# The row bias, the sum's epsilon and half of the top-k comparisons of the first fourteen attention units, moved to GpSimd

## The chip, the core and the metric

One Trainium2 chip, one core. The metric is the device time of one execution in microseconds (us). A core has a matrix engine (TensorE; its matmuls are "PE" in the profile, its weight loads "PEld"), a vector engine (VectorE, "DVE"), an engine for activation functions (ScalarE, "ACT"), a general-purpose engine (GpSimd, "POOL") and an engine that here only issues transfers (SyncE, "SP"). Each takes its instructions in order; an instruction that waits holds up everything behind it on its engine. Arrays are tiles of 128 partitions times a number of elements.

## What is computed

Three stages in a chain: attention that keeps the 32 largest scores of each row, a mixture of eight experts weighted by a Sinkhorn-balanced gate, and a second feed-forward with a Mish-like activation. Only the first concerns the change:

```python
scores = scale * (q @ k.T)                      # 2 batches, 8 heads, 576 x 576, head size 64
kth = np.partition(scores, -32)[..., -32:-31]   # 32nd largest of each row
scores = np.where(scores >= kth, scores, -1e9)
attn = np.exp(scores - scores.max(-1))
attn = attn / (attn.sum(-1) + 1e-9)
x = attn @ v                                    # then experts, then the second feed-forward
```

## The kernel before

The 1152 rows (two batches of 576) are nine token tiles of 128. A **unit** is one tile and one head, 72 in all; units 0 to 7 are tile 0, units 8 to 15 are tile 1, and so on. The expert stage runs in three chunks of tiles, (0, 1), (2, 3) and (4 to 8), so it can begin when unit 15 is done; what it needs of later tiles is computed beside it.

A unit goes through five steps. `scores` multiplies on TensorE into one PSUM tile and ScalarE copies it to `s` (L235). `threshold` finds the 32 largest of each row on VectorE: four times MAX8 (L254, eight largest into `top`) with three MATCH_REPLACE8 between (L261, which strike those eight out of the copy `w`). `mask` and the exponential follow in one of two ways. The units after the first `POOL_UNITS` = 13 take the exponential of the raw scores early, and one VectorE instruction (L290) compares, multiplies and sums. The first 13 units, called pooled here, take the other way:

- VectorE writes -3e38 where a score is below the 32nd largest, else 0 (L285, the comparison).
- GpSimd adds the scores to it (L286).
- VectorE multiplies the row's maximum by -0.125 into `nb` (L271, the bias), one number per partition.
- ScalarE takes the exponential with that bias and sums the row into `sm` (L272).

`norm` adds 1e-9 to the sum on VectorE (L299), takes the reciprocal on VectorE (L300), and ScalarE scales the row (L305). `values` transposes on TensorE, copies on ScalarE (L328, L339), multiplies by the values, and after a tile leaves `xh`/`xl`, the two parts of the expert stage's input (L362 to L367).

The small tiles `top`, `nb`, `sm` and `r` have four buffers each: the bias of unit u+4 can be written when the exponential of unit u has read its own. `s` has six buffers, `em` three pairs.

TensorE's order is written out by hand: at step i of `attention` the scores of unit i come first, then the values of unit i-5 for a pooled unit (i-4 for the others), then two units of early scores of tiles 2, 3, 5 and 6, whose halves ScalarE copies out (L239). So the scores of unit u+6 stand on TensorE behind the values of unit u. The order on the other engines is set by a planner from stream priorities and its own estimates of when each operand is ready. Two streams matter: what stands in `moe` comes behind `attn` (L299 and L300 of pooled units are put there), and weight preparation of the later pieces (`prep`) comes ahead of `attn`.

GpSimd also makes the low parts of keys and queries (L158, L188), clears query tiles (L179), and makes the low parts of the first expert weights (L522), which are loaded ahead and first used when the expert stage begins. Units of tile 2 are held on VectorE until the reciprocal of unit 15 (the "ends" in `threshold` and `norm`).

Of the kernel before, what the change touches and what calls it, by code (L numbers as in the profile page):

```python
# [14 lines left out]
ALU = mybir.AluOpType  # L15
# [20 lines left out]
NEG = -3.0e38  # L36
SCALE = 0.125
EPS = 1e-9
# [5 lines left out]
LAG = 2  # L44
LAG2 = 2
AHEAD = 2
POOL_UNITS = 13
EARLY = [(t, h) for t in (2, 3) for h in range(H)] + [(t, h) for t in (5, 6) for h in range(HG)]
EARLY_FROM, EARLY_PER_STEP = 5, 2
HOLD, RATE = 8, 0.25  # L50
# [22 lines left out]
def attention_moe_moe2(ctx: ExitStack, tc: tile.TileContext, qT, kT, vm, vt, wg, wst, w64, out):  # L73
    nc = tc.nc
# [5 lines left out]
    def after(inst, earlier):  # L80

        tc.add_manual_dep(
            inst.ins,
            earlier.ins.name,
            mybir.DependencyInfo(mybir.DependencyClass.NoSync, mybir.DependencyReason.DATA),
            reason="order",
        )
# [180 lines left out]
    def exponential(t, h, dst, src, eng, **kw):  # L268

        nb = small.tile([P, 1], F32, tag="nb", name=f"nb_{t}_{h}")  # L270
        eng.tensor_scalar(nb, live["top", t, h][:, 0:1], -SCALE, None, op0=ALU.mult)  # L271
        nc.scalar.activation(dst, src, AF.Exp, bias=nb, scale=SCALE, **kw)  # L272
        return dst

    def mask(t, h, on_pool):

        with st("attn"):
            s = live.pop(("s", t, h))
            sm = small.tile([P, 1], F32, tag="sm", name=f"sm_{t}_{h}")
            kth = live["top", t, h][:, TOPK - 1 : TOPK]  # L280
            if h % 2 == 0:
                live["pair", t, h] = sp.tile([P, 2 * S], F32, tag="em", name=f"em_{t}_{h}", bufs=3)
            em = live["pair", t, h - h % 2][:, h % 2 * S :][:, :S]
            if on_pool:
                nc.vector.tensor_scalar(em, s, kth, NEG, op0=ALU.is_lt, op1=ALU.mult)  # L285
                nc.gpsimd.tensor_tensor(em, em, s, ALU.add)  # L286
                exponential(t, h, em, em, nc.vector, accum_out=sm)
            else:
                e = live.pop(("e", t, h))
                nc.vector.scalar_tensor_tensor(em, s, kth, e, op0=ALU.is_ge, op1=ALU.mult, accum_out=sm)  # L290
            live["em", t, h], live["sm", t, h] = em, sm
        yield from ()

    def norm(t, h, on_pool):
        with st("attn"):
            em, sm = live["em", t, h], live.pop(("sm", t, h))
            r = small.tile([P, 1], F32, tag="r", name=f"r_{t}_{h}")
            with st("moe" if on_pool else "attn"):
                nc.vector.tensor_scalar(r, sm, EPS, None, op0=ALU.add)  # L299
                inv = nc.vector.reciprocal(r, r)  # L300
            if (t, h) == (CHUNKS[0][-1], H - 1):
                live["ends"] = inv
                for inst in live.pop("held", ()):
                    after(inst, inv)
            nc.scalar.activation(em, em, AF.Copy, scale=r)  # L305
        yield from ()
# [96 lines left out]
    def attention():  # L403
# [10 lines left out]
        for u, (t, h) in enumerate(units):  # L414
            pooled = u < POOL_UNITS
            for order, (stage, delay) in enumerate(
                (
                    (scores, 0),
                    (partial(threshold, on_pool=pooled), AHEAD),
                    (partial(mask, on_pool=pooled), AHEAD + 1),  # L420
                    (partial(norm, on_pool=pooled), AHEAD + (2 if pooled else 1)),
                    (values, AHEAD + (3 if pooled else 2)),
                )
            ):
                plan.setdefault(u + delay, []).append((order, u, partial(stage, t, h)))
# [420 lines left out]
```

## Time and profile before

| | |
|---|---|
| median of 3 runs | 1249.01 us (1248.32 to 1250.55) |
| the profiled execution's own time | 1249.09 us |
| its span, first to last instruction | 1247.3 us |
| busy over the span | PE 95%, PEld 83%, DVE 69%, ACT 52%, POOL 44% |
| mean granted TensorE clock | 0.993 of full speed |

How to read it: the span has stages. Up to about 107 us there is attention of tiles 0 and 1 alone; from there to about 500 us expert work and the rest of attention run together; then the last expert chunk, and the second feed-forward. Shares over the whole span mix these, so the rows below are taken by stretch. A line such as L285 is a line of the kernel before.

### The profile page before, as it was taken

The numbers are of one execution on the slowest core, as the hardware profiler recorded it, in microseconds if no ns is written. First come the engines' busy times: TensorE is split into PE (matmuls) and PEld (weight loads), VectorE is DVE, ScalarE is ACT, GpSimd is POOL, SyncE is SP. The second block draws the span as 40 slices with busy tenths as digits, with TensorE's granted clock in tenths as the row PEclk, the third lists the DMA queues.
The fourth block names the chain that finished last, engine by engine and source line by source line (L and its number), as shares of the span: only waits on it lengthen the run. The fifth ranks groups of instructions, "written<-read, shape, count | busy, mean of one in ns | idle before, by whom it ended". The sixth has DMA issues, their size and how long they took to land.

```text
span 1247.3 us, 20676 instructions
## 1 busy us (share of the span) xinstructions
PE 1180.1 (95%) x7267; PEld 1040.7 (83%) x7267; DVE 858.7 (69%) x1857; ACT 648.1 (52%) x1289; POOL 546.8 (44%) x424
## 2 busy tenths in 40 slices
PE   3678999999999999999999988999999999999998
PEld 2566888998889888889888777899999998889997
DVE  6999999999999999534899989952333332323221
ACT  6786777877777777653233333332323333444432
POOL 7844778877877777771112211121111212222110
PEclk9899999999999999999999999999999999999999
DMA  8444555575655555673278776632222231223201
GB/s 254 121 144 148 178 168 173 178 223 170 213 178 167 163 155 160 186 219 120 79 249 267 237 217 205 217 100 76 77 76 73 72 110 54 91 93 119 76 27 43
DMA packets 105113, 183.18 MB, mean 147 GB/s; under 512 B 14128, under 2 KB 24624, under 8 KB 105008
## 3 DMA queue, kind: packets, MB, share of 16 engines
q1 hardware_dynamic: 103712, 180.68, 46.6%
q8 instruction: 57, 0.93, 0.3%
q10 hardware_dynamic: 1296, 1.18, 0.3%
q14 instruction: 48, 0.39, 0.1%
HBM read 158.55 MB, written 23.27 MB: 146 GB/s over the span
## 4 chain that ended last, share of the span: by engine, by line
PE 66%; DVE 24%; DMA 6%; issue 2%; POOL 1%; ACT 1%; SPq 0%; POOLq 0%; ACTq 0%; DVEq 0%
PE h_c2e L619 12%; PE y_c2e L596 11%; PE h_d L619 8%; PE y_d L596 8%; PE y_c0e L596 7%; PE h_c0e L619 7%; DVE top L254 6%; DVE w L261 5%; PE h_c1e L619 4%; PE y_c1e L596 3%; DMA cx<-in_w_dram 3%; DVE em L290 2%; DVE acc L640 2%; PE pv L348 2%; PE tr L325 1%
## 5 line engine op out<-in xcount | busy, mean ns | idle before, releaser
L522 POOL TENSOR_TENSOR wl_c2e<-wraw_c2e,wh_c2e 128x512 fp32r<-128x512 f32 x64 | 90.7, 1417 | 358.8 <-ACT wh_c2e L520 332.0
L522 POOL TENSOR_TENSOR wl_c1e<-wraw_c1e,wh_c1e 128x512 fp32r<-128x512 f32 x128 | 172.5, 1372 | 52.4 <-ACT wh_c1e L520 49.3
L522 POOL TENSOR_TENSOR wl_c0e<-wraw_c0e,wh_c0e 128x512 fp32r<-128x512 f32 x128 | 171.6, 1356 | 53.0 <-ACT wh_c0e L520 49.9
L619 PE MATMUL h_c2e<-xh,wh_c2e 128*128 128x320 f32 x512 | 161.3, 315 | 14.4 <-DVE hl_c2e L538 14.2
L520 ACT ACTIVATE wh_c2e<-wraw_c2e 128x512 fp32r<-128x512 f32 x128 | 80.7, 630 | 174.5 <-PE y_c2e L596 110.3
L619 PE MATMUL h_c2e<-xl,wh_c2e 128*128 128x320 f32 x512 | 158.7, 310 | 0.0
L619 PE MATMUL h_c2e<-xh,wl_c2e 128*128 128x320 f32 x512 | 158.5, 310 | 0.0
L254 DVE MAX8 top<-w 128x8 f32<-128x576 f32 x216 | 157.7, 747 | 0.8
L596 PE MATMUL y_c2e<-wh_c2e,hh_c2e 128*128 128x512 f32 x320 | 126.6, 396 | 0.5 <-DVE acc L640 0.5
L596 PE MATMUL y_c2e<-wl_c2e,hh_c2e 128*128 128x512 f32 x320 | 125.7, 393 | 0.0
L596 PE MATMUL y_c2e<-wh_c2e,hl_c2e 128*128 128x512 f32 x320 | 125.2, 391 | 0.0
L538 DVE SCALAR_TENSOR_TENSOR hl_c2e<-h_c2e,hh_c2e 128x320 fp32r<-128x320 f32 x128 | 62.1, 485 | 87.2 <-ACT hh_c2e L537 87.0
L619 PEld LDWEIGHTS h_c2e<-xh,wh_c2e 128*128 128x128 f32 x512 | 96.6, 189 | 24.0 <-DVE hl_c2e L538 21.9
L522 POOL TENSOR_TENSOR wl_d<-wraw_d,wh_d 128x512 fp32r<-128x512 f32 x32 | 41.4, 1293 | 161.0 <-ACT wh_d L520 161.0
L520 ACT ACTIVATE wh_c0e<-wraw_c0e 128x512 fp32r<-128x512 f32 x128 | 80.4, 629 | 51.9 <-PE y_c0e L596 21.0
L261 DVE MATCH_REPLACE8 w<-top,w 128x576 f32<-128x576 f32 x144 | 106.3, 740 | 0.0
L619 PEld LDWEIGHTS h_c2e<-xl,wh_c2e 128*128 128x128 f32 x512 | 96.6, 189 | 1.8
L557 DVE TENSOR_TENSOR hl_d<-mg_d,hh_d 128x320 fp32r<-128x320 f32 (+1 forms) x48 | 31.5, 657 | 95.7 <-ACT hh_d L556 95.7
L619 PEld LDWEIGHTS h_c2e<-xh,wl_c2e 128*128 128x128 f32 x512 | 96.7, 189 | 0.0
L520 ACT ACTIVATE wh_c1e<-wraw_c1e 128x512 fp32r<-128x512 f32 x128 | 79.8, 627 | 27.7 <-PE y_c1e L596 11.3
L522 DVE TENSOR_TENSOR wl_c2e<-wraw_c2e,wh_c2e 128x512 fp32r<-128x512 f32 x64 | 47.7, 745 | 66.0 <-ACT wh_c2e L520 65.9
L520 ACT ACTIVATE wh_d<-wraw_d 128x512 fp32r<-128x512 f32 x64 | 40.4, 631 | 95.8 <-PE y_d L596 40.9
(170 smaller groups left out, 3325.5 us busy)
## 6 DMA issues: line engine op xcount, KB each, us to landing
wraw_c0e<-in_wst_dram SPq DMA_DIRECT2D x128, 256.0 KB, 3.0
wraw_c1e<-in_wst_dram SPq DMA_DIRECT2D x128, 256.0 KB, 3.0
wraw_c2e<-in_wst_dram SPq DMA_DIRECT2D x128, 256.0 KB, 2.9
cx<-in_w_dram SPq DMA_DIRECT2D x32, 512.0 KB, 4.6
wraw_d<-w SPq DMA_DIRECT2D x64, 256.0 KB, 2.7
yd<-ysp SPq DMA_DIRECT2D x32, 256.0 KB, 3.6
yb<-yd SPq DMA_DIRECT2D x32, 256.0 KB, 3.4
w<-cc SPq DMA_DIRECT2D x32, 256.0 KB, 3.2
```

What stands on the lines that cost most here:

```text
L254: top8 = nc.vector.max(g, src)
L261: nc.vector.match_replace(w, g, src, NEG)
L290: nc.vector.scalar_tensor_tensor(em, s, kth, e, op0=ALU.is_ge, op1=ALU.mult, accum_out=sm)
L325: nc.tensor.transpose(tr[:, c, :], em[:, j * D + c * P :][:, :P], ident)
L348: nc.tensor.matmul(pv[i * D : (i + 1) * D, pair, c0:c1], vmain[b, pair][:, i, c, :], live["at", i][:, c, c0:c1], start=(c == 0), stop=False,)
L520: nc.scalar.activation(hi, raw, AF.Copy)
L522: eng.tensor_sub(lo, raw, hi)
L538: nc.vector.scalar_tensor_tensor(l, ps, 0.0, h, op0=ALU.max, op1=ALU.subtract)
L557: nc.vector.tensor_sub(l, g, h)
L596: nc.tensor.matmul(y, h[:, j * P : (j + 1) * P], w, start=(f == 0 and k == 0), stop=(f == nf - 1 and k == 2),)
L619: nc.tensor.matmul(ps, w[:, c * P : (c + 1) * P], x[:, c, c0 : c0 + m], start=(k == 0), stop=(k == 3 * NC - 1),)
L640: nc.vector.scalar_tensor_tensor(acc[t], y, gate[:, t, e : e + 1], acc[t], op0=ALU.mult, op1=ALU.add)
```

## The change

`POOL_UNITS` becomes 14, so unit 13 (tile 1, head 5) takes the pooled way too. In pooled units the bias and the epsilon go to GpSimd, and so does the comparison of even heads; odd heads keep it on VectorE. The reciprocal stays on VectorE, the streams and TensorE's written order stay as they are (the values of unit 13 move from step 17 to step 18).

```diff
-POOL_UNITS = 13
+POOL_UNITS = 14
...
             if on_pool:
-                nc.vector.tensor_scalar(em, s, kth, NEG, op0=ALU.is_lt, op1=ALU.mult)
+                flags = nc.vector if h % 2 else nc.gpsimd
+                flags.tensor_scalar(em, s, kth, NEG, op0=ALU.is_lt, op1=ALU.mult)
                 nc.gpsimd.tensor_tensor(em, em, s, ALU.add)
-                exponential(t, h, em, em, nc.vector, accum_out=sm)
+                exponential(t, h, em, em, nc.gpsimd, accum_out=sm)
...
             with st("moe" if on_pool else "attn"):
-                nc.vector.tensor_scalar(r, sm, EPS, None, op0=ALU.add)
+                (nc.gpsimd if on_pool else nc.vector).tensor_scalar(r, sm, EPS, None, op0=ALU.add)
                 inv = nc.vector.reciprocal(r, r)
```

## Rows read from the trace of the kernel before

**Rows 1.** The page: share of the chain that ended last, by engine.
```profile
PE 66%; DVE 24%; DMA 6%; issue 2%; POOL 1%; ACT 1%; SPq 0%; POOLq 0%; ACTq 0%; DVEq 0%
```

**Rows 2.** Busy time by stretch: stretch, length, busy us (count) of each engine, clock, DMA.
```profile
7.30:107.60 100.30, 62.43 (x372) 49.10 (x373) 96.14 (x240) 76.20 (x169) 63.45 (x51) 0.93 0.57 175
107.60:488.00 380.40, 377.61 (x2798) 337.46 (x2797) 374.78 (x906) 283.66 (x556) 294.89 (x221) 1.00 0.56 173
```

**Rows 3.** Waits of TensorE from 107.6 us on: total, times, longest.
```profile
PE h_c2e L619 <- DVE hl_c2e L538: 14.2, 16, 2.0
```

**Rows 4.** The chain that ended last, 40 to 56 us: start, us, what.
```profile
41.64 0.77 ACT em L272 x2
...
42.44 0.15 DVE nb L271
```

**Rows 5.** Groups on VectorE, 7.3 to 107.6 us: count | busy, mean ns | idle before.
```profile
L254 DVE MAX8 top<-s 128x8 f32<-128x576 f32 x16 | 11.9, 746 | 3.1 <-ACT s L235 2.9
...
L285 DVE TENSOR_SCALAR em<-s,top 128x576 f32<-128x576 f32 x13 | 8.9, 687 | 0.0
...
L290 DVE SCALAR_TENSOR_TENSOR em<-s,top,e 128x576 f32<-128x576 f32 x3 | 2.4, 802 | 0.0
...
L271 DVE TENSOR_SCALAR nb<-top 128x1 f32<-128x1 f32 x17 | 2.3, 140 | 3.0 <-ACT em L272 3.0
...
L299 DVE TENSOR_SCALAR r<-sm 128x1 f32<-128x1 f32 x16 | 2.2, 137 | 0.0
```

**Rows 6.** VectorE in order of time: start, us, instruction, [idle before].
```profile
25.98 0.15 DVE L271 TENSOR_SCALAR nb<-top 128x1 f32<-128x1 f32 x1 [2.68 <-ACT em L272]
...
37.29 0.70 DVE L285 TENSOR_SCALAR em<-s,top 128x576 f32<-128x576 f32 x1
...
60.79 0.76 DVE L254 MAX8 top<-s 128x8 f32<-128x576 f32 x1
61.47 0.07 DVE L261 MATCH_VALUE_LOAD w<-top,w 128x8 f32 x1
61.53 0.74 DVE L261 MATCH_REPLACE8 w<-top,w 128x576 f32<-128x576 f32 x1
62.19 0.08 DVE L261 MATCH_VALUE_LOAD w<-top,s 128x8 f32 x1
...
62.92 0.14 DVE L271 TENSOR_SCALAR nb<-top 128x1 f32<-128x1 f32 x1
62.98 1.41 DVE L254 MAX8 top<-w 128x8 f32<-128x576 f32 x2
64.30 0.14 DVE L299 TENSOR_SCALAR r<-sm 128x1 f32<-128x1 f32 x1
64.36 0.52 DVE L285 TENSOR_SCALAR em<-s,top 128x576 f32<-128x576 f32 x1
64.78 0.09 DVE L261 MATCH_VALUE_LOAD w<-top,w 128x8 f32 x1
```

**Rows 7.** ScalarE in order of time: the copy of unit 9's scores.
```profile
60.11 0.65 ACT L235 ACTIVATE s<-sc 128x576 f32<-128x576 f32 x1
```

**Rows 8.** Busy time by stretch, as in rows 2, within the first stage.
```profile
7.30:25.30 18.00, 6.62 (x20) 4.91 (x20) 14.87 (x33) 8.84 (x16) 13.61 (x12) 1.00 0.89 263
25.30:55.00 29.70, 16.87 (x82) 13.25 (x84) 28.73 (x69) 23.70 (x52) 28.85 (x21) 0.91 0.60 179
55.00:107.60 52.60, 38.95 (x274) 30.94 (x271) 52.53 (x139) 43.66 (x103) 21.00 (x18) 0.92 0.44 143
```

**Rows 9.** GpSimd in order of time: the addition of unit 3.
```profile
44.52 1.65 POOL L286 TENSOR_TENSOR em<-em,s 128x576 f32<-128x576 f32 x1
```

**Rows 10.** Groups on GpSimd, 7.3 to 107.6 us, as in rows 5.
```profile
L286 POOL TENSOR_TENSOR em<-em,s 128x576 f32<-128x576 f32 x13 | 19.0, 1461 | 8.8 <-DVE em L285 6.4 <-DVE r L299 2.3
...
L522 POOL TENSOR_TENSOR wl_c0e<-wraw_c0e,wh_c0e 128x512 fp32r<-128x512 f32 x9 | 11.8, 1333 | 1.4 <-ACT wh_c0e L520 1.1
L179 POOL MEMSET qraw<- 128x512 f32 x4 | 2.1, 528 | 0.1
...
L411 POOL TENSOR_TENSOR wgs<-wgraw,wgs 128x32 fp32r<-128x32 f32 x1 | 0.3, 252 | 0.1
```

## The prediction

> **What bounds the kernel now.** I read the chain that ended last first: 66% of the span on TensorE, 24% on VectorE, GpSimd 1% [rows 1]. Then busy time by stretch, since these shares mix stages. Up to 107.6 us, before the first expert matmul, VectorE is busy 96.14 of 100.30 us and TensorE 62.43: VectorE sets the pace. From 107.6 to 488 us TensorE is busy 377.61 and VectorE 374.78 of 380.40, so both are full there [rows 2]. After 107.6 us the largest wait of TensorE is 14.2 us in 16 pieces, all on VectorE's low parts in the last expert chunk [rows 3]. Nothing in the later stages waits for a fixed moment, so what the first stage gains or loses should pass to the end one for one, and the question is by how much unit 15 ends earlier.
>
> Inside the first stage I read the engines by thirds. VectorE is nearly full in the last two (28.73 of 29.70 and 52.53 of 52.60). GpSimd is full as well from 25.3 to 55 us, 28.85 of 29.70, and only 21.00 of 52.60 afterwards [rows 8]. And the chain goes, at 42.44 us, from ScalarE's exponential to VectorE's bias [rows 4]: VectorE was waiting there, for a buffer of the bias that the exponential four units earlier was still to read.
>
> **What leaves VectorE.** The durations overlap by some hundredths, so I cost by the distance to the next start, and between 60.79 and 64.78 us every kind is to be seen: a bias 0.06 us (62.92 to 62.98), an epsilon 0.06 (64.30 to 64.36), a comparison 0.42 against a duration of 0.52 [rows 6].
> - Bias: 14 units (unit 13 included) by 0.06 = 0.84 us. Epsilon: 14 by 0.06 = 0.84 us.
> - Comparisons of even heads: units 0, 2, 4, 6, 8, 10, 12, seven by the group's mean of 0.687 less 0.10 of overlap = 4.1 us [rows 5, 6].
> - Unit 13 loses its combined instruction, 0.802 less some 0.08 of overlap, and gets a comparison of 0.42: 0.3 us [rows 5, 6].
> - VectorE waits 3.0 us in front of biases, 2.68 of it at 25.98 us, when the bias of unit 4 waits for unit 0's exponential [rows 5, 6]. The wait moves to GpSimd with the bias; VectorE goes on to the comparison of unit 1, which needs nothing from it: 3.0 us.
>
> Together 9.1 us by which VectorE could be ahead. This is a gross figure. What is late next is the arrival of scores.
>
> **What of it can be used.** VectorE works on several units at a time; this hides late scores. The stock runs down, however. Unit 9's scores are copied out at 60.11 + 0.65 = 60.76 us [rows 7], and VectorE takes them at 60.79 [rows 6]. What it still has of unit 8 then is one MATCH_REPLACE8 with its load (61.47 to 62.19, 0.72) and one of the two MAX8 at 62.98 (0.66): 1.4 us, apart from the comparison. So if unit 9's scores come no earlier than now, a VectorE that is ahead does these 1.4 us before, and then idles. After that point it saves only what is still to come: biases of units 9 to 13, 0.30; epsilons of 7 to 13, 0.42; comparisons of units 8, 10, 12 at 0.42 = 1.26; unit 13, 0.3. That is 2.3, and with the 1.4 it makes 3.7 us. The lead is therefore 3.7 us with the scores of unit 9 standing still, 9.1 at most if they come early enough, and less by every us that they come later.
>
> **What is added to GpSimd, and whether the scores stand still.** Scores of unit u+6 stand behind the values of unit u on TensorE, and these need GpSimd's addition. In 25.3 to 55 us GpSimd has no room: unit 3's comparison ends on VectorE at 37.99 and its addition starts at 44.52 [rows 6, 9], behind other work of the queue. Into this stretch come two comparisons (units 2 and 4; unit 0's falls before 25.3 us, where GpSimd is idle 4.4 of 18.0 us), five biases and five epsilons.
> - One comparison on GpSimd is not in the trace. Below it lies a write-only fill, 0.528 us for 512 elements, 0.59 for 576; above it the two-input addition of the same size, 1.461 [rows 10]. One input is read, two operations are done: I take 1.0, and as a far bound twice the addition, 2.9.
> - A 128x1 operation: at most 0.252, that of 128x32 [rows 10]; at least what VectorE takes, 0.06 [rows 6]. I take 0.2.
>
> That is 2 x 1.0 + 10 x 0.2 = 4.0 us more in a full queue (1.8 to 8.3 by the bounds). Against it, VectorE hands the comparison of unit 1 over 2.7 us earlier and that of unit 3 some 3 to 4 us earlier, and nine weight preparations, 11.8 us [rows 10], stand in this stage though the first is used at 107.6 us; the planner can let them give way. I take these as equal: the scores of unit 9 stay where they are. After 55 us GpSimd has 31 us of idle time, which hides the other comparisons, the small work and unit 13's addition; without that cover each comparison of an even unit would put its 1.0 us less VectorE's 0.42 into the way from threshold to addition. A wait is new there: GpSimd's bias waits for an exponential, and its epsilon for a sum, with key parts and additions queued behind them; VectorE's reciprocal waits for GpSimd. Against the epsilon's place on VectorE I count this at zero, from -1 to +2 us.
>
> One page of the Trainium skill, SBUF — State Buffer, section "Who interferes with whom", says that a VectorE instruction in a two-port mode and a GpSimd instruction exclude each other for the whole instruction. The trace agrees in kind: the comparison takes 0.52 at 64.36 and 0.687 in the mean [rows 5, 6]. By that rule the seven comparisons left on VectorE would meet more GpSimd work; were each 0.2 us longer, the sum would fall by 1.4 us to 2.3.
>
> **The sum.** The profiled execution took 1249.09 us, 0.08 above the median, with 1.8 outside its span. 1249.09 - 3.7 = 1245.4; against the median 1245.3. I predict 1245.3.
>
> **The rivals.**
> A. My forecast: scores of unit 9 within about 2 us of now, 1243 to 1247.5. Chance 0.40.
> B. The scores come early too: weight preparation gives way, and the earlier comparisons pull exponentials, values and scores with them. For it speaks that VectorE was tied with the chain at 42 us [rows 4]; against it GpSimd's full queue [rows 8]. The whole 9.1 us: 1240.0. Chance 0.20.
> C. The added 4.0 us push every addition of the full stretch by as much: 3.7 - 4.0 = -0.3 us, 1249.4, no change. Chance 0.22.
> D. GpSimd becomes the bound of the first 60 us because its comparison is dear. At the far bound 2 x 2.9 + 10 x 0.25 = 8.3 us, and 3.7 - 8.3 = -4.6: 1253.7, slower. It decides from the point where the added work passes 3.7 + 2.5 us, a comparison of 2.1 us. For it: GpSimd's two-input operation already takes 1.461 where VectorE's one-input comparison takes 0.52. Against it: the fill takes 0.528, and only one input is read. Chance 0.18. The Trainium skill, GPSIMD Engine Reference, section "Engine selection", would have elementwise work on VectorE, though it calls one-input work on GpSimd about as fast as the line allows; its section "Elementwise — side-by-side cycle accounting" puts data-dependent branching at some 12 cycles an element at 1.2 GHz, which for 576 elements would be, as an estimate, 5.8 us a comparison and, by the same sum, about 10 us more time than now. No row here shows a comparison on GpSimd.
>
> **How the numbers follow.** Below 0.2%, 2.5 us, this kernel can't be told from unchanged. Faster: B, most of A, 0.56 together; same: the rest of A, most of C, 0.25; slower: most of D and a little of C, 0.19. The range from 1239.5 to 1252 takes in B, A, C and the nearer part of D. Within the likeliest case it is 1243 to 1247.5.
>
> **What would show it.** Right: seven comparisons left on VectorE and no wait in front of a bias; seven on GpSimd at about 1.0 us each; VectorE idle a few us in front of first MAX8s between 45 and 65 us; the first expert matmul 3 to 4 us before 107.6, and every later stage shifted by as much. Case B: VectorE without idle time and the first expert matmul near 98.5 us. Case C: GpSimd full to about 59 us and the first expert matmul where it is. Case D: a comparison of over 2.1 us. The prediction fails on its premise if the expert stage starts earlier and the end does not follow, for instance because the planner orders the later stages differently.

## The result, and the profile after

The changed kernel takes 1267.68 us (median of 4 runs, 1264.81 to 1268.74) against 1249.78 beside it: ratio 1.014, 95% interval [1.0118, 1.0162]. It is 17.5 us slower; the forecast was 1245.3, with a range from 1239.5 to 1252. Here and below a difference in us is the ratio less one, times the median of the kernel before in the same comparison. One slow execution each of two runs below (1496.92 and 2957.98 us) is left out of their ratios. Rows of a trace are those of one execution, which in the runs below took up to 4.4 us more or less than the median of its kernel, so differences of a few us between two traces can be chance. In the changed kernel every line from 286 on has a number one higher: the comparison is L286, the addition L287, the epsilon L300, the reciprocal L301, the low part L523.

The first look is where the stage ends. The first expert matmul, in TensorE's order of time (start, us, instruction), before and after:

```profile
107.63 0.37 PE L619 MATMUL h_c0e<-xh,wh_c0e 128*128 128x256 f32 x1
```
```profile
124.72 0.37 PE L620 MATMUL h_c0e<-xh,wh_c0e 128*128 128x256 f32 x1
```

That is 17.1 us later, and the span grew from 1247.3 to 1264.9, by 17.6: the loss arises in the first stage and passes on. The second look is busy time by stretch, as in [rows 8]:

```profile
7.30:25.30 18.00, 6.64 (x20) 4.90 (x20) 17.05 (x34) 9.26 (x16) 15.47 (x17) 1.00 0.87 267
25.30:55.00 29.70, 9.41 (x51) 7.55 (x51) 22.99 (x46) 16.99 (x34) 28.58 (x24) 0.97 0.49 155
55.00:107.60 52.60, 33.50 (x211) 27.91 (x211) 38.92 (x86) 38.20 (x90) 34.41 (x40) 0.76 0.26 86
```

From 25.3 to 55 us GpSimd (last of the five busy times) is full, as before, and every other engine has fallen: VectorE from 28.73 to 22.99, TensorE from 16.87 to 9.41. After 55 us GpSimd does 34.41 in place of 21.00. TensorE's granted clock (the first number behind the busy times) is 0.76 there in place of 0.92; whether that is a cause is taken up with the experiments. The page's shares of the chain that ended last, which answer to [rows 1], have GpSimd at 4% for 1%:

```profile
PE 61%; DVE 24%; DMA 7%; POOL 4%; issue 2%; ACT 1%; SPq 0%; POOLq 0%; ACTq 0%
```

In order of time that chain is on GpSimd, with gaps for issue only, from 27.49 to 66.2 us. In [rows 4] it had gone over to VectorE at 42.44.

The new operations, as groups on GpSimd up to 130 us (count | busy, mean ns | idle before), and the comparisons left on VectorE up to 117 us:

```profile
L287 POOL TENSOR_TENSOR em<-em,s 128x576 f32<-128x576 f32 x14 | 19.6, 1409 | 3.1 <-DVE em L286 2.6
L286 POOL TENSOR_SCALAR em<-s,top 128x576 f32<-128x576 f32 x7 | 15.9, 2265 | 0.7 <-DVE top L254 0.2
...
L300 POOL TENSOR_SCALAR r<-sm 128x1 f32<-128x1 f32 x14 | 3.2, 227 | 5.7 <-ACT em L272 4.2 <-PE sc L226 0.8
L271 POOL TENSOR_SCALAR nb<-top 128x1 f32<-128x1 f32 x14 | 3.1, 225 | 3.8 <-DVE top L254 3.1
```
```profile
L286 DVE TENSOR_SCALAR em<-s,top 128x576 f32<-128x576 f32 x7 | 6.1, 867 | 0.1
```

A comparison takes 2.27 us on GpSimd, longer than the addition of two inputs. What it does to the queue is read on GpSimd in order of time:

```profile
28.86 2.50 POOL L523 TENSOR_TENSOR wl_c0e<-wraw_c0e,wh_c0e 128x512 fp32r<-128x512 f32 x2
31.44 1.40 POOL L158 TENSOR_TENSOR ks<-kraw,ks 64x576 fp32r<-64x576 f32 x1
32.92 3.81 POOL L523 TENSOR_TENSOR wl_c0e<-wraw_c0e,wh_c0e 128x512 fp32r<-128x512 f32 x3
36.81 1.41 POOL L158 TENSOR_TENSOR ks<-kraw,ks 64x576 fp32r<-64x576 f32 x1
38.30 0.21 POOL L271 TENSOR_SCALAR nb<-top 128x1 f32<-128x1 f32 x1
38.57 0.21 POOL L300 TENSOR_SCALAR r<-sm 128x1 f32<-128x1 f32 x1
38.88 2.24 POOL L286 TENSOR_SCALAR em<-s,top 128x576 f32<-128x576 f32 x1
...
52.63 2.76 POOL L287 TENSOR_TENSOR em<-em,s 128x576 f32<-128x576 f32 x2
...
59.57 2.42 POOL L286 TENSOR_SCALAR em<-s,top 128x576 f32<-128x576 f32 x1
61.96 1.26 POOL L188 TENSOR_TENSOR q<-qraw,q 128x512 fp32r<-128x512 f32 x1
63.31 0.24 POOL L271 TENSOR_SCALAR nb<-top 128x1 f32<-128x1 f32 x1
63.61 0.22 POOL L300 TENSOR_SCALAR r<-sm 128x1 f32<-128x1 f32 x1
```

and ScalarE beside it (unit 0's sum, unit 2's exponential, unit 8's scores; the copy of unit 8's scores before stands below):

```profile
30.30 0.19 ACT L272 ACTIVATION_READ_ACCUMULATOR em<-em,nb 128x1 f32 x1
...
55.42 0.78 ACT L272 ACTIVATE em<-em,nb 128x576 f32<-128x576 f32 x1 [2.61 <-POOL em L287]
...
72.31 0.66 ACT L235 ACTIVATE s<-sc 128x576 f32<-128x576 f32 x1
```
```profile
52.22 0.63 ACT L235 ACTIVATE s<-sc 128x576 f32<-128x576 f32 x1
```

Follow two units. Unit 0's sum is there at 30.49, and its epsilon, 0.21 us of work, runs at 38.57: ahead of it in the queue stand low parts of expert weights first used after 107 us, two key parts and a bias. Unit 2's comparison runs at 38.88; its addition is the second of the pair at 52.63, so it ends at 55.39. Before, the addition ended at 40.49, and the epsilon ran on VectorE at 42.51:

```profile
39.08 1.41 POOL L286 TENSOR_TENSOR em<-em,s 128x576 f32<-128x576 f32 x1
```
```profile
42.51 0.14 DVE L299 TENSOR_SCALAR r<-sm 128x1 f32<-128x1 f32 x1
```

The addition is 14.9 us later. The epsilon then comes at 63.61, behind a key part, unit 4's addition, a comparison, two query parts and a bias. So it is 21.1 us late, 14.9 by the addition and 6.2 by what comes after it, and unit 2's scaled row starts 19.7 us late, at 64.12 for 44.44. The scores of unit 8, which TensorE does behind the values of unit 2, are in SBUF at 72.97 for 52.9 before: 20.1 late. The waits of VectorE and of TensorE, 7.3 to 117 us (total, times, longest), say the same from the other side; the last row is TensorE's wait before:

```profile
DVE r L301 <- POOL r L300: 12.6, 7, 4.0
DVE top L254 <- ACT s L235: 9.4, 6, 2.4
```
```profile
PE tr L326 <- ACT em L306: 32.8, 3, 19.0
```
```profile
PE tr L325 <- ACT em L305: 14.9, 6, 8.1
```

TensorE's wait for the scaled row grew by 17.9, the size of the loss.

### The profile page after: what moved, and what is told of

Its sections match the earlier page's. It is cut to its first block, busy times and chain, and to the rows that moved or that the text cites. A ratio compares the mean times of both kernels' runs of the same rounds, so it can differ in the third digit from the quotient of the medians.

```text
span 1264.9 us, 20684 instructions
## 1 busy us (share of the span) xinstructions
PE 1179.6 (93%) x7267; PEld 1041.4 (82%) x7267; DVE 859.1 (68%) x1821; ACT 650.6 (51%) x1290; POOL 568.6 (45%) x460
## 4 chain that ended last, share of the span: by engine, by line
PE 61%; DVE 24%; DMA 7%; POOL 4%; issue 2%; ACT 1%; SPq 0%; POOLq 0%; ACTq 0%
PE h_c2e L620 11%; PE y_c2e L597 10%; PE h_d L620 8%; PE y_d L597 8%; PE h_c0e L620 7%; PE y_c0e L597 6%; DVE top L254 5%; DVE w L261 5%; DMA cx<-in_w_dram 4%; PE y_c1e L597 3%; DVE em L291 3%; PE h_c1e L620 2%; PE pv L349 2%; DMA yb<-yd 2%; DVE acc L641 2%
## 5 line engine op out<-in xcount | busy, mean ns | idle before, releaser
L523 POOL TENSOR_TENSOR wl_c2e<-wraw_c2e,wh_c2e 128x512 fp32r<-128x512 f32 x64 | 93.3, 1459 | 353.9 <-ACT wh_c2e L521 322.9
L523 POOL TENSOR_TENSOR wl_c1e<-wraw_c1e,wh_c1e 128x512 fp32r<-128x512 f32 x128 | 171.9, 1366 | 54.3 <-ACT wh_c1e L521 51.2
L523 POOL TENSOR_TENSOR wl_c0e<-wraw_c0e,wh_c0e 128x512 fp32r<-128x512 f32 x128 | 169.5, 1335 | 57.1 <-ACT wh_c0e L521 54.0
L620 PE MATMUL h_c2e<-xh,wh_c2e 128*128 128x320 f32 x512 | 161.2, 315 | 12.6 <-DVE hl_c2e L539 12.4
L620 PEld LDWEIGHTS h_c2e<-xh,wh_c2e 128*128 128x128 f32 x512 | 96.6, 189 | 21.8 <-DVE hl_c2e L539 19.7
L523 POOL TENSOR_TENSOR wl_d<-wraw_d,wh_d 128x512 fp32r<-128x512 f32 x32 | 41.4, 1293 | 161.0 <-ACT wh_d L521 161.0
L523 DVE TENSOR_TENSOR wl_c2e<-wraw_c2e,wh_c2e 128x512 fp32r<-128x512 f32 x64 | 48.1, 752 | 65.0 <-ACT wh_c2e L521 64.9
```

Of the source, the lines that this page charges most:

```text
L523: eng.tensor_sub(lo, raw, hi)
L620: nc.tensor.matmul(ps, w[:, c * P : (c + 1) * P], x[:, c, c0 : c0 + m], start=(k == 0), stop=(k == 3 * NC - 1),)
```

## The experiments

The accounts to be told apart: the loss is GpSimd's added time (the comparison is simply long); it is one misplaced part, the epsilon above all; or it is order, that is, short and urgent operations standing in one queue behind long ones that nobody waits for. The marker "first expert matmul" is 107.63 in the kernel before.

**One part alone.** Epsilon on GpSimd:

```diff
-                nc.vector.tensor_scalar(r, sm, EPS, None, op0=ALU.add)
+                (nc.gpsimd if on_pool else nc.vector).tensor_scalar(r, sm, EPS, None, op0=ALU.add)
```

> Only the epsilon of the 13 pooled units is on GpSimd; bias and comparisons stay on VectorE. Three theories of the 18 us. Price: GpSimd's comparison takes 2.24 us and fills it; then this kernel, without it, is within 2.5 us of before (1247 to 1251). Epsilon: its 0.2 us stands behind 1.3 to 1.4 us operations in GpSimd's queue and VectorE's reciprocal waits (12.6 us of such waits in the changed kernel); then this alone costs 8 us or more (1257 to 1265). Order: the addition of an even unit is placed far behind its comparison (unit 2's 12.8 us later); then this is near before as well, up to 4 us slower.

Measured: 1255.33 against 1248.82, ratio 1.0049 [1.0034, 1.0063], +6.1 us; first expert matmul 113.67. On ScalarE unit 1's sum is there at 32.00, and on GpSimd, in order of time:

```profile
31.82 0.18 ACT L272 ACTIVATION_READ_ACCUMULATOR em<-em,nb 128x1 f32 x1
```
```profile
32.23 4.03 POOL L522 TENSOR_TENSOR wl_c0e<-wraw_c0e,wh_c0e 128x512 fp32r<-128x512 f32 x3
36.34 1.40 POOL L158 TENSOR_TENSOR ks<-kraw,ks 64x576 fp32r<-64x576 f32 x1
37.81 1.37 POOL L522 TENSOR_TENSOR wl_c0e<-wraw_c0e,wh_c0e 128x512 fp32r<-128x512 f32 x1
39.26 0.21 POOL L299 TENSOR_SCALAR r<-sm 128x1 f32<-128x1 f32 x1
```

An operation of 0.21 us comes 7.3 us after its operand. The loss lies between the two branches that were expected, below the 8 us of the epsilon's and above the 2.5 and 4 us of the others. It is more than the thirteen operations last, some 3 us together. Unit 7's scores, behind the values of unit 1, are at 51.1 for 46.8.

The bias on GpSimd:

```diff
-                exponential(t, h, em, em, nc.vector, accum_out=sm)
+                exponential(t, h, em, em, nc.gpsimd, accum_out=sm)
```

> Only the bias of the 13 pooled units is on GpSimd. All three theories (price, epsilon, order) put little here. My prediction's own term says 3.0 us of waits and 0.8 us of work leave VectorE: 1246 to 1249. If the wait for the exponential four units earlier merely stops GpSimd in VectorE's stead, 1250 to 1253.

Measured: 1251.07, ratio 1.0014 [1.0002, 1.0026], +1.7 us; first expert matmul 109.61. A small loss, in the range expected if the wait merely moves: VectorE now waits 4.4 us in front of epsilons, for 3.0 in front of biases before.

The comparison of even heads on GpSimd:

```diff
-                nc.vector.tensor_scalar(em, s, kth, NEG, op0=ALU.is_lt, op1=ALU.mult)
+                flags = nc.vector if h % 2 else nc.gpsimd
+                flags.tensor_scalar(em, s, kth, NEG, op0=ALU.is_lt, op1=ALU.mult)
```

> Only the comparison of the seven even pooled units is on GpSimd. Price: 2 x 2.24 us more in the full stretch up to 55 us, 4 to 6 us slower than before at most, with additions right behind their comparisons. Order: additions of units 2 and 4 again stand several operations behind their comparisons, and this alone brings most of the loss, 1259 to 1268. Epsilon: within 3 us of before.

Measured: 1260.19, ratio 1.0084 [1.0065, 1.0103], +10.5 us, in the range expected of order; first expert matmul 119.79. GpSimd in order of time, comparisons of units 2 and 4 and additions of units 3 and 2:

```profile
39.94 2.21 POOL L286 TENSOR_SCALAR em<-s,top 128x576 f32<-128x576 f32 x1
42.12 1.42 POOL L287 TENSOR_TENSOR em<-em,s 128x576 f32<-128x576 f32 x1
...
47.85 2.20 POOL L286 TENSOR_SCALAR em<-s,top 128x576 f32<-128x576 f32 x1
50.14 1.40 POOL L158 TENSOR_TENSOR ks<-kraw,ks 64x576 fp32r<-64x576 f32 x1
51.61 1.40 POOL L287 TENSOR_TENSOR em<-em,s 128x576 f32<-128x576 f32 x1
```

Unit 2's addition starts 9.5 us after its own comparison has ended on the same engine, behind unit 3's addition, two low parts, unit 4's comparison and two key parts.

Fourteen units in place of thirteen:

```diff
-POOL_UNITS = 13
+POOL_UNITS = 14
```

> Only the number of pooled units, 13 to 14; all operations stay where they were. No theory puts any of the loss here: 1247 to 1251.

Measured: 1250.94, ratio 1.001 [0.9995, 1.0025], +1.2 us, not told from none. The four alone add to 6.1 + 1.7 + 10.5 + 1.2 = 19.5, all together cost 17.5.

**One part taken back.** The changed kernel with the epsilon on VectorE (the first diff, reversed):

> The changed kernel with the epsilon alone back on VectorE. If the parts add up (epsilon 6.1, bias 1.8, comparisons 10.5, unit 13 1.3 us by the single edits), 1260 to 1263. If the epsilon is what turns the waits of the others into a stop, because VectorE's reciprocal waits for it in order, 1250 to 1257.

Measured: 1259.63, ratio 1.0078 [1.0054, 1.0102], +9.7; first expert matmul 118.84. So the epsilon accounts for 7.8 of the 17.5 us. The 9.7 that are left are about what the comparison cost alone.

**The order of the additions.** The comparison alone, with GpSimd's additions in order of units:

```diff
...
-                nc.gpsimd.tensor_tensor(em, em, s, ALU.add)
...
+                add = nc.gpsimd.tensor_tensor(em, em, s, ALU.add)
+                if "added" in live:
+                    after(add, live["added"])
+                live["added"] = add
```

> Only the comparisons of even units on GpSimd (the run that took 1260.2), with GpSimd's additions made to follow in the order of the units, so that unit 2's addition comes before unit 3's. Order: half or more of the 10.5 us comes back, 1249 to 1255. Full queue: the additions still stand five operations behind their comparisons, unit 2's barely moves, and so do the scores of unit 8: 1257 to 1262.

Measured: 1260.26, ratio 1.008 [1.0055, 1.0104], +10.0. Swapped additions are not the cause. Put in order, the additions of units 2 and 3 stand as a pair at 50.22 us, and unit 2's still starts 8.1 us after its comparison has ended at 42.11.

**Low parts out of the way.** The changed kernel with the low parts of the first expert's weights ordered behind the addition of unit 7, and the kernel before with the same (`live["add7"]` is that addition):

```diff
...
-            eng.tensor_sub(lo, raw, hi)
+            low = eng.tensor_sub(lo, raw, hi)
+            if tag.startswith("c0e0"):
+                after(low, live["add7"])
```

> The changed kernel, with the first expert's low weight parts held on GpSimd until the addition of unit 7; same operations, other order. Full queue: GpSimd has no room up to 64 us because 9 to 10 low parts of 1.3 us stand among the additions, epsilons and comparisons; without them the additions of units 2 and 4 come right behind their comparisons and most of the 18 us comes back, 1246 to 1256. Price: each comparison is 2.24 us and its time, not its place, is what costs; then 1262 to 1268.

> The kernel before with the same low weight parts held until the addition of unit 7. If GpSimd's full queue from 25 to 55 us already held back scores there, 1 to 4 us faster than before. If VectorE alone sets the pace of the first stage, as the prediction read it, unchanged, 1247 to 1251. If ScalarE or the transfers suffer from the delay, slower.

Measured: changed 1262.24, ratio 1.0099 [1.0077, 1.0121], +12.4; before 1251.11, ratio 1.0021 [1.0004, 1.0037], +2.6. So the full queue did not hold back the kernel before: room in it brought no gain. In the changed kernel units 8 and 10 now get their scores at 52.4 and 62.8 us, ahead of the kernel before, and then the row of low parts comes, with unit 6's epsilon and unit 8's comparison behind it:

```profile
59.63 7.48 POOL L525 TENSOR_TENSOR wl_c0e<-wraw_c0e,wh_c0e 128x512 fp32r<-128x512 f32 x6
67.19 0.21 POOL L302 TENSOR_SCALAR r<-sm 128x1 f32<-128x1 f32 x1
67.50 2.24 POOL L286 TENSOR_SCALAR em<-s,top 128x576 f32<-128x576 f32 x1
```

The loss had moved, not gone. The same, held behind the addition of unit 12 (`add12` in place of `add7`):

> The changed kernel with the first expert's low weight parts held on GpSimd until the addition of unit 12 rather than of unit 7. In the run held until unit 7 the scores of unit 10 were ready at 62 us, 2 us ahead of the kernel before, and then six low parts in one row (7.5 us) stood ahead of unit 6's epsilon and unit 8's comparison. Full queue: without that row most of the loss goes, 1245 to 1256. Price: the comparisons' 2.24 us each cost by themselves; no better than the run held until unit 7, 1259 to 1266.

> The kernel before with the low weight parts held until the addition of unit 12. If GpSimd's queue already cost the kernel before, 1242 to 1247. If VectorE alone set its pace, 1247 to 1251. If the low parts then come too late for the first expert matmuls, 1252 to 1260; this would also bound what the same hold can give the changed kernel.

Measured: changed 1259.21, ratio 1.0082 [1.0061, 1.0104], +10.2; before 1252.15, ratio 1.0037 [1.0023, 1.0051], +4.6. Unit 15's scores are at 90.0, as in the kernel before (91.0), yet the first expert matmul is at 118.97: six low parts stand on GpSimd from 89.24 for 7.67 us, and behind them and two query parts stand an epsilon, until 99.45, and an addition:

```profile
89.24 7.67 POOL L525 TENSOR_TENSOR wl_c0e<-wraw_c0e,wh_c0e 128x512 fp32r<-128x512 f32 x6
...
99.45 0.22 POOL L302 TENSOR_SCALAR r<-sm 128x1 f32<-128x1 f32 x1
```

This run also speaks against TensorE's clock as the cause: the granted clock was 0.94 and 0.91 in the stretches from 25.3 to 55 and from 55 to 107.6 us, for 0.91 and 0.92 in the kernel before, and the first expert matmul was still 11.3 us late. So the low parts were held behind everything that is urgent, with unit 13's epsilon as the last:

```diff
...
+                eps = (nc.gpsimd if on_pool else nc.vector).tensor_scalar(r, sm, EPS, None, op0=ALU.add)
+                if (t, h) == (1, 5):
+                    live["add12"] = eps
...
+                after(low, live["add12"])
```

> The changed kernel with the low weight parts held on GpSimd until unit 13's epsilon, the last of GpSimd's work for pooled units. With the hold until unit 12's addition the scores came as early as in the kernel before (unit 15's at 90.0 against 91.0 us) and 10 us were lost after that, where a row of low parts stood ahead of unit 13's addition and the last epsilons. Full queue: with that row moved behind them, the first expert matmul comes at 108 to 113 us and the time is 1249 to 1255. Price of the comparison by itself: still 1257 to 1262.

Measured: 1250.77 against 1249.33, ratio 1.0004 [0.9992, 1.0016], +0.5. GpSimd's groups are the changed kernel's, the comparison among them as long:

```profile
L286 POOL TENSOR_SCALAR em<-s,top 128x576 f32<-128x576 f32 x7 | 15.7, 2240 | 1.0 <-DVE r L303 0.3 <-DVE top L254 0.2
```

and the first expert matmul is back:

```profile
107.76 0.56 PE L624 MATMUL h_c0e<-xh,wh_c0e 128*128 128x256 f32 x1
```

This decides whether length alone or order makes the loss: with the same operations at the same durations, and only the low parts elsewhere in the queue, 17.0 of 17.5 us are gone. It is not a gain that any kernel has from holding the low parts, since the two other holds cost the kernel before 2.6 and 4.6 us. The 0.5 that is left is a net figure, though: what left VectorE is in it, and the kernel before with this very hold was not run. The traced execution took 1247.08, 3.7 less than its kernel's median.

The end of the stage says where the rest of the expected gain may be. VectorE starts unit 15's combined instruction 4.1 us before the kernel before (102.66). Meanwhile GpSimd makes the low parts in a row, and ScalarE stands in front of a weight conversion whose load waits for them, with unit 15's copy (L331) behind it (from 80 to 112 us the queue of these loads waited for low parts 9 times, 6.5 us in all):

```profile
98.53 1.10 DVE L291 SCALAR_TENSOR_TENSOR em<-s,top,e 128x576 f32<-128x576 f32 x1
```
```profile
95.27 7.97 POOL L525 TENSOR_TENSOR wl_c0e<-wraw_c0e,wh_c0e 128x512 fp32r<-128x512 f32 x6
```
```profile
104.66 0.63 ACT L523 ACTIVATE wh_c0e<-wraw_c0e 128x512 fp32r<-128x512 f32 x1 [1.03 <-DMA wraw_c0e<-in_wst_dram]
105.20 0.58 ACT L331 ACTIVATE at<-tr 128x512 f32<-128x512 f32 x1
```

**The comparison's place and size.** Only the comparisons of units 8, 10 and 12 on GpSimd:

```diff
+                flags = nc.gpsimd if (t and h % 2 == 0) else nc.vector
...
```

> The kernel before with only the comparisons of units 8, 10 and 12 on GpSimd, after 60 us, where GpSimd is idle more than half the time. Full queue: nothing to stand behind; VectorE loses 3 x 0.42 us of work: 1246 to 1251. Price: 2.24 us in place of 0.42 on the way from threshold to addition in each, 4 to 6 us slower, 1253 to 1255.

Measured: 1250.9, ratio 1.0023 [1.0011, 1.0035], +2.9. Here GpSimd has room (27.38 of 52.60 us busy), and the loss is still clear, 1.4 to 4.4 us. The three comparisons together last 5.4 us longer than 0.42 each, on the way from threshold to addition. So length costs something by itself. Three of seven comparisons cost 2.9 of 10.5 us; if the parts add, the four of tile 0 cost the other 7.6.

Even heads split, 288 columns on each engine:

```diff
...
+                    nc.gpsimd.tensor_scalar(em[:, :288], s[:, :288], kth, NEG, op0=ALU.is_lt, op1=ALU.mult)
+                    nc.vector.tensor_scalar(em[:, 288:], s[:, 288:], kth, NEG, op0=ALU.is_lt, op1=ALU.mult)
```

> The kernel before with the comparison of even units split, the first 288 columns on GpSimd and the other 288 on VectorE. If GpSimd's time in the queue is what costs (1260.2 with all 576 columns there), about half of the 10.5 us remains, 1252 to 1256. If a place behind other work costs whatever the size of the operation, as with the 0.2 us epsilon, most of it remains, 1256 to 1261.

Measured: 1253.29, ratio 1.0036 [1.0025, 1.0048], +4.5, 43% of the whole comparison's cost. This is the branch in which GpSimd's time in the queue counts: with a mean of 1.31 for 2.2 us on GpSimd, less than half of the loss remains. Order and length work together: in the rows above, an urgent operation comes late by the sum of what stands ahead of it. The group on GpSimd up to 117 us:

```profile
L288 POOL TENSOR_SCALAR em<-s,top 128x288 f32<-128x288 f32 x7 | 9.2, 1310 | 5.8 <-DVE top L254 2.8 <-ACT em L309 2.8
```

**Is VectorE's time in the first stage worth anything?** Eight bias buffers in the kernel before, so that no bias waits for an exponential:

```diff
-        nb = small.tile([P, 1], F32, tag="nb", name=f"nb_{t}_{h}")
+        nb = small.tile([P, 1], F32, tag="nb", name=f"nb_{t}_{h}", bufs=8)
```

> The kernel before with eight buffers for the bias in place of four, so that VectorE no longer waits for the exponential four units earlier; no work moves. The prediction's term: 3.0 us of waits gone, of which 3.0 or nothing passes on. If VectorE sets the pace of the first stage, 1245 to 1247. If the scores set it, the wait only moves to the next first MAX8, 1247.5 to 1250.

Measured: 1252.42, ratio 1.0017 [1.0005, 1.0029], +2.1; first expert matmul 108.48. The 3.0 us of waits in front of biases are gone, and 3.2 us in front of scores (before: 2.9) and 1.6 in front of an epsilon stand there: they bought nothing.

The kernel before without the epsilon, in all 72 units (the reciprocal reads the sum, so 1e-9 is not added):

```diff
-                nc.vector.tensor_scalar(r, sm, EPS, None, op0=ALU.add)
-                inv = nc.vector.reciprocal(r, r)
+                inv = nc.vector.reciprocal(r, sm)
```

> The kernel before without the epsilon of 1e-9 (left out in all 72 units; each sum is at least 1): the reciprocal reads the sum. This takes work from VectorE and adds none anywhere. If a hundredth saved on VectorE passes to the end where VectorE is full, 72 x 0.06 = 4.3 us less, 1243 to 1247; if scores set the pace of the first stage, only part, 1246 to 1250.

Measured: 1244.86 against 1248.43, ratio 0.9971 [0.9958, 0.9984], -3.6. The first expert matmul is at 107.64: in this trace nothing of it was gained in the first stage. Both together:

> The kernel before without the epsilon (3.6 us faster than before) and with eight buffers for the bias. If the buffers are worth their 3.0 us, 1241 to 1243; if not, 1244 to 1246.

Measured: 1251.57, ratio 1.0024 [1.0012, 1.0036], +3.0. The buffers cost here as well; why was not looked into.

**Spreading the low parts.** The changed kernel, the k-th low part behind the epsilon of unit 5 + k:

```diff
...
+                k = live["lows"] = live.get("lows", -1) + 1
+                after(low, live["eps", min(5 + k, POOL_UNITS - 1)])
```

> All parts of the change, with the nine low parts of the first expert's weights spread over GpSimd's order: the k-th of them behind the epsilon of unit 5 + k (at most 13). With all nine behind unit 13's epsilon VectorE was done with unit 15's combined instruction at 98.53 + 1.10 = 99.6 us, 3.9 before the kernel before (102.66 + 0.82 = 103.5), but ScalarE then stood 1.6 and 1.0 us in front of weight conversions whose loads wait for a buffer that a low part frees, with unit 15's copy behind them. If that account is right, spreading gives back 2 to 4 us: first expert matmul at 104 to 106 us, 1245 to 1247.5 us. If instead any low part between the small operations costs its 1.3 us, as the row of six did, the first expert matmul is at 108 to 113 and the time 1250 to 1255.

Measured: 1249.92 against 1248.25, ratio 1.0008 [0.9994, 1.0022], +1.0; first expert matmul 111.77. The gain did not come. That the end of the stage alone had taken it back is not borne out; between the small operations the low parts cost again: unit 15's scores are at 92.8 us, where they were at 88.5 with all low parts behind the last epsilon. The marker is 4.1 us late and the span of the same trace only 1.4 longer (1248.7): here the loss did not pass on one for one, and the runs don't say why.

The same without the epsilon in all 72 units, the k-th low part behind the addition of unit 6 + k:

> The same with the epsilon left out in all 72 units (the reciprocal reads the sum itself), and the k-th low part behind the addition of unit 6 + k (at most 13). GpSimd is rid of 14 operations of 0.23 us and of the wait for each sum, VectorE of 58 by 0.06 = 3.5 us. If both gains hold: 1240 to 1244 us, first expert matmul at 103 to 106. If the low parts between the additions cost as much as they did in a row: 1247 to 1252, first expert matmul at 108 to 113.

Measured: 1241.38 against 1248.25, ratio 0.9943 [0.9926, 0.9961], -7.1 us, the best of all. First expert matmul:

```profile
106.93 0.37 PE L623 MATMUL h_c0e<-xh,wh_c0e 128*128 128x256 f32 x1
```

It keeps bias and comparisons on GpSimd, and unit 15's scores are at 87.9 for 91.0. It beats both kernels. The first expert matmul is only 0.7 us earlier, so most of the gain comes later. Leaving the epsilon out gave the kernel before 3.6 us by itself; if the parts add, the moved work and the spreading are worth the other 3.5, and the intervals of both runs are wide.

## Why the prediction was wrong

**What held.** The premise did: 17.1 us in the first stage, 17.6 in the span. So did the count of operations, and the 128x1 operation, 0.2 taken and 0.225 measured. The comparisons left on VectorE got longer: those of units 1, 3, ... 11 took 0.66 us in the mean before and 0.93 after, where the prediction's side sum put 0.2 us on each. The Trainium skill, SBUF — State Buffer, section "Who interferes with whom", says that a VectorE instruction in a two-port mode and a GpSimd instruction block each other; the trace agrees in kind.

**"I take 1.0" for a comparison.** It took 2.24 to 2.27, within the bounds of 0.59 to 2.9 and past the 2.1 from which rival D decides. I went by the nearness of a one-input operation to a fill; the addition, 1.461 [rows 10], was the nearer row, and too short as well. The estimate of 5.8 us that I drew from the Trainium skill, GPSIMD Engine Reference, section "Elementwise — side-by-side cycle accounting" (some 12 cycles an element for data-dependent branching), was 2.6 times too long.

**Rival D had the engine right and the price wrong.** With the measured durations its sum is 2 x 2.24 + 10 x 0.225 = 6.7, less 3.7: 3.0 us slower. The time was 17.5 slower. D charged the added time once, and most of the loss is not that time: with the low parts behind everything the same operations cost 0.5 us net. The time is not free either, as the three late comparisons (2.9 us) and the halved ones (43% of the loss) show.

**The step that failed: "the planner can let them give way. I take these as equal: the scores of unit 9 stay where they are."** They came at 79.6 us in place of 60.8. Weight preparation is ahead of attention in the planner's priorities, which I had written down, and it didn't give way. What each moved operation releases was therefore late by the queue ahead of it: unit 0's epsilon by 8.1 us, unit 2's addition by 14.9. The earlier handovers by VectorE, which I set against it, are worthless when the receiver is the full queue. Scores of unit u+6 stand behind the values of unit u, so a delay of unit 2 is a delay of unit 8, and of all behind it.

**"Against the epsilon's place on VectorE I count this at zero, from -1 to +2 us."** Alone it cost 6.1 us [4.2 to 7.9]. I named what is queued behind the waiting epsilon, not what is queued ahead of it. On VectorE it stands among instructions of 0.7 us, on GpSimd behind rows of 1.3 us each.

**The gross 9.1 us.** The waits of 3.0 us were worth nothing (eight buffers, no gain), and no worth of the epsilon's time on VectorE shows in this stage (the first expert matmul stayed at 107.64 without it). The pace was set by when scores arrive, which the prediction saw for unit 9 and then took as fixed. The 3.7 us aren't refuted, and not shown: with the low parts behind everything VectorE ended unit 15's instruction at 99.63 for 103.48, 3.9 us earlier, in one execution that was itself 3.7 faster than the median, and the stage's tail took it back there. Spreading the low parts didn't release it, with unit 15's scores later again; what would release it stays open.

## What to carry over

Before moving a short operation to an engine with room on average, list what stands ahead of it in that engine's order in its own stretch, and who waits for what it releases; 0.2 us of work can cost 6. When a queue is full, ask which of its work nobody needs yet: moving that was worth 17 us here. And take away what needn't be done rather than moving it: without the epsilon, and with the low parts spread, the same idea is 7.1 us faster than the kernel before, and 3.6 of this the kernel before has from leaving out the epsilon alone.

## What was not expected of the hardware

On GpSimd a comparison and multiplication by constants of one 128x576 input took 2.2 to 2.4 us, 2.24 in the median, and 1.31 in the mean for 288 columns: as an estimate from these two, 3.2 ns a column and some 0.4 us beside it. The addition of two such inputs took 1.41. On VectorE the same comparison took 0.50 us at its shortest. An operation on 128x1 lasts 0.20 to 0.40 us on GpSimd, mostly 0.21 to 0.23, and starts 0.3 us before the next (38.57 to 38.88), against 0.06 on VectorE [rows 6].
